# Fused cosine attention and feed-forward on one core: a ramp by quads of heads transposed on TensorE, dense chunks of 384 and 512 tokens, and each pair weighed one visit earlier

## The chip, the cores and the metric

The kernel runs on one core of a Trainium2 chip. Times are device microseconds (us) of that core. A profile's span is about 2 us shorter than the time of the run, because it counts from the first to the last instruction. Ratios are the mean time of one kernel's fast runs over that of the other's fast runs of the same rounds, so they are not quite the ratio of the medians quoted beside them.

## The reference, cut to what matters

```python
# q, k, v: (8, 12, 448, 64): batches, heads, tokens, head size; tau = 0.1
q_n = q / (norm(q) + 1e-6);  k_n = k / (norm(k) + 1e-6)
attn = softmax(q_n @ k_n.T / tau)
x = (attn @ v), heads joined              # (3584, 768)
h = x @ w_in                              # w_in (768, 2048)
out = maximum(0.01 * h, h) @ w_out        # w_out (2048, 768)
```

## The kernel before

For each batch the kernel loads q, k and v as bf16, sums squares on VectorE, takes the root on ScalarE as a logarithm and an exponential, inverts on VectorE, scales on GpSimd, and transposes q and k by DMA. Attention goes by six pairs of heads. A *visit* computes half the scores of a pair and their exponentials. *Weighing* a pair multiplies the exponentials by ones (the sums) and by v; VectorE takes the reciprocal and multiplies into x. The *dense* work is layer 1 (16 groups of matmuls for each batch) and layer 2 (56 groups in all). It is meant to fill TensorE while the next batch's attention waits for ScalarE and VectorE.

The order of all this is static. A scheduler with a clock of its own deals dense groups into the visits, and each engine then works its own list in that order:

```python
    def fill(us):
        end = clock[0] + us
        while at[0] < len(dense) and clock[0] < end:
            work, took, b = dense[at[0]]
            if done.get(b, 1e9) + 6.0 > clock[0]:   # b's attention must be over for 6 us
                break
            work(); clock[0] += took; at[0] += 1

    def prepare(b, step):            # the next batch
        if step == 0:   norm_sums(b, "q")                     # VectorE
        elif step == 1: norm_root(b, "q"); norm_sums(b, "k")  # ScalarE, VectorE
        elif step == 2: norm_inverse(b, "q"); norm_root(b, "k")
        elif step == 3: norm_inverse(b, "k"); ...scale q on GpSimd
        elif step == 4: turn(b, "q"); ...scale k on GpSimd
        elif step == 5: turn(b, "k")
        elif step == 6 and b + 1 < B: load(b + 1, "q"); load(b + 1, "k")
        elif step == 11 and b + 1 < B: load(b + 1, "v")

    last = None
    for b in range(B):
        for p in range(HP):
            for half in range(2):
                scores(b, p, half)                   # visit n = 2 * p + half
                clock[0] += 0.5
                if half == 1:
                    if last is not None:
                        weigh(*last)                 # the pair before, two visits late
                        ...
                    last = (b, p)
                prepare(b + 1, 2 * p + half)
                fill(3.0)
    # ... (functions that build the pieces, the ramp and the end are cut)
```

The last pair of batch b-1 is weighed at visit 1 of batch b, and the sums of q of batch b+1 are listed at visit 0. In VectorE's list these sums come ahead of the reciprocal of that last pair, so VectorE can do them early, while TensorE still has dense work.

## Time and profile before

| | before |
|---|---|
| time, median of 3 | 557.13 us (555.75 to 560.46) |
| span of the profile | 553.5 us |
| TensorE busy | 446.2 us (81%) |
| first score matmul | 62.7 us |
| first layer-1 matmul | 119.0 us |

These are lines of the page of the kernel before: busy time, and the span in 40 slices of 13.8 us, in tenths.

```profile
PE 446.2 (81%) x2816; PEld 216.5 (39%) x2816; DVE 265.8 (48%) x163; ACT 260.0 (47%) x409; POOL 118.3 (21%) x131
...
PE   0000285589999999499999996799999997999996
...
DVE  3600769963862536825834356836742338350000
...
PEclk9999999789999999679999999799999999999999
```

TensorE (PE) does nothing for four slices, works partly until slice 10, and is then full, except for holes about 120 us apart. In the first two of these holes the granted clock falls too. Next, what TensorE waited for, by the table of waits (us in total, times, longest):

```profile
PE sc L131 <- DMA kT<-k_n: 64.6, 2, 62.7
PE sc L131 <- ACT pe L135: 37.7, 46, 5.4
PE sm L146 <- DVE rs L153: 0.2, 1, 0.2
```

The first wait is the ramp: scores need the transposed k. No dense matmul ever waits for an eviction. The timeline of one hole (start, duration, engine, what; in brackets the idle time before it and what ended it):

```profile
217.07 0.34 ACT L93 ACTIVATE q_ni<-q_ni,tiny 112x48 f32<-112x48 f32 x1
...
221.84 3.35 DVE L87 TENSOR_REDUCE k_ni<-k_n 112x48 f32<-112x3072 bf16 x1
...
225.29 0.33 ACT L93 ACTIVATE k_ni<-k_ni,tiny 112x48 f32<-112x48 f32 x1 [5.99 <-DVE q_ni L98]
...
226.75 0.56 PE L131 MATMUL sc<-qT,kT 64*128 64x448 bf16 x2 [5.41 <-ACT pe L135]
...
238.84 4.76 PE L164 MATMUL mm<-xT,w_in_sb 128*128 128x448 bf16 x18
```

The root of k (the logarithm at L93) sat 6 us at the head of ScalarE's list, until the sum of k was done on VectorE (L87, over at 225.2; the bracket names L98, a short operation that VectorE ended at the same moment). The exponentials behind it could not start, and TensorE's scores waited 5.4 us for them. The sum of q had been done beforehand: its root ran without a wait. Dense work came back at 238.84.

### The profile page before, as it was taken

The page shows a single profiled execution, that of the slowest core. Times are in us where ns is not written, and L with a number is a line of the kernel's source. Part 1 is how long each engine was busy: PE and PEld are TensorE (multiplying, and loading weights), DVE is VectorE, ACT ScalarE, POOL GpSimd, SP SyncE. Part 2 cuts the span into 40 slices and gives each one's busy share as a digit, 9 for nine tenths or more (in the row PEclk, how much of TensorE's full clock was granted, in tenths as well). Part 3 has the DMA queues.
Part 4 walks back from the last instruction along what each step waited for, and adds up shares of the span by engine and source line. Part 5 has one row for each costly group of instructions (what it writes and reads, how often), then busy time and mean ns, then how long its engine had stood idle before and what let it go on. Part 6 is the DMA issues. An engine that isn't in the chain of part 4 may idle for free.

```text
span 553.5 us, 6672 instructions
## 1 busy us (share of the span) xinstructions
PE 446.2 (81%) x2816; PEld 216.5 (39%) x2816; DVE 265.8 (48%) x163; ACT 260.0 (47%) x409; POOL 118.3 (21%) x131
## 2 busy tenths in 40 slices
PE   0000285589999999499999996799999997999996
PEld 0000032234554454144544453244544553455553
DVE  3600769963862536825834356836742338350000
ACT  0000466467447534555546543666457437632421
POOL 3430090280055000630072000900440000000000
PEclk9999999789999999679999999799999999999999
DMA  9999829448149423392449025290560110002013
GB/s 139 216 201 188 109 54 146 50 89 114 15 103 152 67 58 76 62 138 32 73 83 167 14 66 99 51 150 1 108 128 1 40 51 25 2 1 71 16 28 86
DMA packets 83518, 45.26 MB, mean 82 GB/s; under 512 B 44832, under 2 KB 79136, under 8 KB 83488
## 3 DMA queue, kind: packets, MB, share of 16 engines
q0 software_dynamic: 35488, 22.81, 29.1%
q1 hardware_dynamic: 48000, 22.03, 19.7%
q8 instruction: 22, 0.36, 0.3%
q14 instruction: 8, 0.07, 0.0%
HBM read 45.61 MB, written 11.01 MB: 102 GB/s over the span
## 4 chain that ended last, share of the span: by engine, by line
PE 73%; DVE 9%; DMA 8%; ACT 5%; SPq 2%; POOL 1%; issue 1%; ACTq 0%; DVEq 0%; POOLq 0%
PE mm L164 27%; PE mm L180 27%; PE sm L146 7%; DMA kT<-k_n 7%; PE sc L131 6%; PE po L146 6%; ACT pe L135 5%; DVE k_ni L87 2%; DVE rs L153 2%; SPq L114 2%; DMA q_bf<-in_q_dram 1%; DVE k_n L86 1%; DVE q_ni L87 1%; POOL k_n L103 1%; DVE q_n L86 1%
## 5 line engine op out<-in xcount | busy, mean ns | idle before, releaser
L153 DVE RECIPROCAL rs<-sm 128x448 f32<-128x448 f32 x48 | 141.8, 2953 | 180.9 <-PE sm L146 180.9
L135 ACT ACTIVATE pe<-sc 112x896 bf16<-112x896 f32 x192 | 163.2, 918 | 60.9 <-PE sc L131 60.9
L164 PE MATMUL mm<-xT,w_in_sb 128*128 128x448 bf16 x768 | 153.9, 355 | 0.0
L180 PE MATMUL mm<-w_out_sb,hT 128*128 128x384 bf16 x896 | 150.1, 326 | 0.0
L131 PE MATMUL sc<-qT,kT 64*128 64x448 bf16 x384 | 62.7, 383 | 102.4 <-DMA kT<-k_n 64.6
L180 PEld LDWEIGHTS <-hT 128*128 128x128 bf16 x896 | 85.9, 98 | 63.2 <-issue 7.6
L168 ACT ACTIVATE hT<-mm 128x448 bf16<-128x448 f32 x128 | 69.8, 545 | 76.4 <-PE mm L164 76.4
L164 PEld LDWEIGHTS <-w_in_sb 128*128 128x128 bf16 x768 | 72.3, 98 | 78.2 <-issue 15.9
L185 ACT COPY osb<-mm 128x384 f32<-128x384 f32 x56 | 26.7, 477 | 110.2 <-PE mm L180 98.6
L131 PEld LDWEIGHTS <-kT 64*128 64x128 bf16 x384 | 15.0, 96 | 147.3 <-issue 81.2
L103 POOL TENSOR_TENSOR q_n<-q_bf,q_ni 112x512 bf16<-112x512 bf16 x42 | 42.3, 1038 | 80.9 <-DVE q_ni L99 80.9
L103 POOL TENSOR_TENSOR k_n<-k_bf,k_ni 112x512 bf16<-112x512 bf16 (+1 forms) x43 | 50.6, 1209 | 22.8 <-DVE k_ni L99 22.8
L146 PE MATMUL sm<-pe,ones 112*64 112x448 bf16 x384 | 51.5, 395 | 0.2 <-DVE rs L153 0.2
L146 PE MATMUL po<-pe,v_bf 112*64 112x448 bf16 x384 | 50.0, 387 | 0.0
L76 POOL DMA_DIRECT2D v_bf<-in_v_dram x8 | 7.5, 935 | 187.4 <-PE sc L131 104.0
L156 DVE TENSOR_TENSOR xT<-po,rs 128x448 bf16<-128x448 f32 x48 | 30.0, 625 | 5.4 <-PE mm L180 0.5
L86 DVE TENSOR_TENSOR q_n<-q_bf 112x3072 bf16<-112x3072 bf16 x8 | 14.0, 1751 | 37.5 <-DMA q_bf<-in_q_dram 37.5
L146 PEld LDWEIGHTS <-v_bf 112*64 112x64 bf16 x384 | 24.1, 121 | 18.1 <-issue 5.3
L146 PEld LDWEIGHTS <-ones 112*64 112x64 bf16 x384 | 19.3, 117 | 25.2 <-issue 18.9
L87 DVE TENSOR_REDUCE k_ni<-k_n 112x48 f32<-112x3072 bf16 x8 | 26.8, 3353 | 0.3
L87 DVE TENSOR_REDUCE q_ni<-q_n 112x48 f32<-112x3072 bf16 x8 | 26.8, 3353 | 0.3
L86 DVE TENSOR_TENSOR k_n<-k_bf 112x3072 bf16<-112x3072 bf16 x8 | 13.9, 1743 | 3.1 <-DMA kT<-k_n 3.1
(22 smaller groups left out, 45.4 us busy)
## 6 DMA issues: line engine op xcount, KB each, us to landing
q_bf<-in_q_dram POOLq DMA_DIRECT2D x8, 672.0 KB, 11.0
k_bf<-in_k_dram POOLq DMA_DIRECT2D x8, 672.0 KB, 13.4
v_bf<-in_v_dram POOLq DMA_DIRECT2D x8, 672.0 KB, 7.4
w_in_sb<-in_moe_w_in_dram POOLq DMA_DIRECT2D x1, 3072.0 KB, 26.3
w_out_sb<-in_moe_w_out_dram POOLq DMA_DIRECT2D x1, 3072.0 KB, 43.7
out_dram<-osb SPq DMA_DIRECT2D x8, 336.0 KB, 3.8
out_dram<-osb SPq DMA_DIRECT2D x8, 288.0 KB, 2.6
out_dram<-osb SPq DMA_DIRECT2D x8, 240.0 KB, 2.8
```

What stands on the lines that cost most here:

```text
L86: nc.vector.tensor_mul(sq, x, x)
L87: nc.vector.tensor_reduce(ni, sq, axis=AX.X, op=ALU.add)
L103: eng.tensor_tensor(out=xn[:, :, h0:h1, :].rearrange("p t h d -> p h t d"), in0=x[:, h0:h1], in1=ni[:, h0:h1].unsqueeze(3).to_broadcast([P ...
L131: nc.tensor.matmul(out=sc[:, a, :S], lhsT=kT[r, o : o + 128], rhs=q4[r, :, p, :], start=True, stop=True,)
L135: nc.scalar.activation(out=pe[:, ki], in_=sc[:PK, :, :S], func=ACTF.Exp, scale=inv_tau)
L146: nc.tensor.matmul(out=dst[64 * a : 64 * a + 64, :], lhsT=ones[:PK, :] if ones_ else vb[:, 2 * p + a, ki, :], rhs=pe[:, ki, a, :], start=( ...
L153: nc.vector.reciprocal(rs, sm)
L156: nc.vector.tensor_mul(st["x", b][:, p, :], po, rs)
L164: nc.tensor.matmul(out=pm[:, :S], lhsT=w_in_sb[:, kt, m * 128 : (m + 1) * 128], rhs=xT[:, kt, :], start=(kt == 0), stop=(kt == KT - 1),)
L168: nc.scalar.activation(out=hT[:, m, (b % 2) * S : (b % 2 + 1) * S], in_=pm[:, :S], func=ACTF.Prelu, alpha=0.01,)
L180: nc.tensor.matmul(out=po[:, :NH], lhsT=hT[:, m, i * 128 : (i + 1) * 128], rhs=w_out_sb[:, m, n * NH : (n + 1) * NH], start=(m == 0), stop ...
L185: nc.scalar.copy(out=osb[:, n * NH : (n + 1) * NH], in_=po[:, :NH])
```

## The change

There are three parts. **Ramp**: batch 0 is loaded by quads of heads, and batches 0 and 1 are normalised by quads and transposed pair by pair on TensorE, with an identity matrix; weights come in pieces; q and k loads have three shared buffers. **Chunks**: layer 1 takes 384 tokens of an even batch and 512 with the odd one, so that layer 2's tiles of 128 tokens fit whole chunks. **Order**: a pair is weighed one visit earlier, and a chunk may start 2 us, not 6, after its attention on the scheduler's clock.

```diff
 # ramp (cut)
+    make_identity(nc, ident)
+    for g in range(G):
+        for what in "qk":
+            load(0, what, 4 * g, 4 * g + 4)
+    load(0, "v")
+    prepare_quad(0, 0, nc.vector, nc.vector)     # norms of one quad
+    load(1, "q")
+    turn_pair(0, 0)                              # 8 TensorE transposes, 2 VectorE copies
+    turn_pair(0, 1)
+    visit(0, 0, 0)
+    ...
 # chunks
+    first = [7 * (c // 2) + 3 * (c % 2) for c in range(B + 1)]
+    def layer1(c, m):
+        n = 128 * (first[c + 1] - first[c])      # 384 or 512 tokens
 # order
-            if done.get(b, 1e9) + 6.0 > clock[0]:
+            if done.get(b, 1e9) + 2.0 > clock[0]:
 ...
-                if half == 1:
-                    if last is not None:
-                        weigh(*last)
-                    last = (b, p)
-                prepare(b + 1, 2 * p + half)
+                if owed:
+                    weigh(*owed.pop(0))
+                if half == 1:
+                    owed.append((b, p))
+                prepare(b + 1, n)                # b == 1 has its own list, n - 4
                 fill(3.0)
 # steps of prepare: the same up to 5, but scaling on GpSimd is listed one step earlier
 # (q at 2, k at 3); loads of q, k, v now at 6, 7 and 8
```

More of the change, by code (lines that the diff above doesn't have):

```diff
@@ L6 @@
 from concourse._compat import with_exitstack
+from concourse.masks import make_identity
 F32 = mybir.dt.float32
@@ L38 @@
     HP = H // 2
+    G = H // 4
     KT = DM // 128
@@ L46 @@
     inp = ctx.enter_context(tc.tile_pool(name="inp", bufs=1))
+    bfpool = ctx.enter_context(tc.tile_pool(name="bfpool", bufs=3))
     vpool = ctx.enter_context(tc.tile_pool(name="vpool", bufs=2))
@@ L50 @@
     wk = ctx.enter_context(tc.tile_pool(name="wk", bufs=2))
+    epool = ctx.enter_context(tc.tile_pool(name="epool", bufs=4))
+    opool = ctx.enter_context(tc.tile_pool(name="opool", bufs=4))
     xpool = ctx.enter_context(tc.tile_pool(name="xpool", bufs=2))
@@ L53 @@
     psc = ctx.enter_context(tc.tile_pool(name="psc", bufs=2, space=bass.MemoryType.PSUM))
-    ppv = ctx.enter_context(tc.tile_pool(name="ppv", bufs=1, space=bass.MemoryType.PSUM))
+    ppv = ctx.enter_context(tc.tile_pool(name="ppv", bufs=2, space=bass.MemoryType.PSUM))
     pmm = ctx.enter_context(tc.tile_pool(name="pmm", bufs=2, space=bass.MemoryType.PSUM))
@@ L62 @@
     nc.vector.memset(tiny, 1e-19)
+    ident = cpool.tile([PK, PK], BF16, name="ident")
     w_in_sb = cpool.tile([128, KT, FF], BF16, name="w_in_sb")
@@ L68, with load @@
     out_r = out.rearrange("(b p t) n -> b t p n", p=PK, t=NT)
+    w_in_r = moe_w_in.rearrange("(ko ki) n -> ki ko n", ki=128)
+    w_out_r = moe_w_out.rearrange("(mo mi) n -> mi mo n", mi=128)
     st = {}
-    def load(b, what):
+    def load(b, what, h0=0, h1=H):
         src = {"q": q_r, "k": k_r, "v": v_r}[what]
-        pool = vpool if what == "v" else inp
-        x = pool.tile([PK, H, NT, D], BF16, name=f"{what}_bf")
-        nc.gpsimd.dma_start(out=x, in_=src[b])
-        st[what, b] = x
@@ L79, in norm_sums @@
-    def norm_sums(b, what):
-        x = st[what, b]
-        xn = inp.tile([PK, NT, H, D], BF16, name=f"{what}_n")
-        ni = small.tile([PK, H, NT], F32, name=f"{what}_ni")
-        sq = xn.rearrange("p t h d -> p (t h d)").rearrange(
-            "p (h t d) -> p h t d", h=H, t=NT
-        )
-        nc.vector.tensor_mul(sq, x, x)
-        nc.vector.tensor_reduce(ni, sq, axis=AX.X, op=ALU.add)
-        st[what + "n", b] = xn
-        st[what + "i", b] = ni
-    def norm_root(b, what):
-        ni = st[what + "i", b]
+        if (what, b) not in st:
+            if what == "v":
+                st[what, b] = vpool.tile([PK, H, NT, D], BF16, name="v_bf")
+            else:
+                st[what, b] = bfpool.tile([PK, H, NT, D], BF16, name="qk_bf")
@@ new lines, in load, with load_w_in, load_w_out, norm_sums @@
+        nc.gpsimd.dma_start(out=st[what, b][:, h0:h1], in_=src[b][:, h0:h1])
+    def load_w_in(i):
+        n = slice(i * FF // 4, (i + 1) * FF // 4)
+        nc.gpsimd.dma_start(out=w_in_sb[:, :, n], in_=w_in_r[:, :, n])
+    def load_w_out(n):
+        nc.gpsimd.dma_start(
+            out=w_out_sb[:, :, n * NH : (n + 1) * NH], in_=w_out_r[:, :, n * NH : (n + 1) * NH]
+        )
+    def norm_sums(b, what, g0=0, g1=G):
+        if (what + "n", b) not in st:
+            st[what + "n", b] = inp.tile([PK, G, NT, 4, D], BF16, name=f"{what}_n")
+            st[what + "i", b] = small.tile([PK, H, NT], F32, name=f"{what}_ni")
+        x, xn, ni = st[what, b], st[what + "n", b], st[what + "i", b]
+        h0, h1 = 4 * g0, 4 * g1
+        sq = xn[:, g0:g1].rearrange("p g t h d -> p (g t h d)").rearrange(
+            "p (h t d) -> p h t d", h=h1 - h0, t=NT
+        )
+        nc.vector.tensor_mul(sq, x[:, h0:h1], x[:, h0:h1])
+        nc.vector.tensor_reduce(ni[:, h0:h1], sq, axis=AX.X, op=ALU.add)
@@ L93, in norm_root, with norm_inverse, norm_apply @@
+    def norm_root(b, what, g0=0, g1=G):
+        ni = st[what + "i", b][:, 4 * g0 : 4 * g1]
         nc.scalar.activation(ni, ni, func=ACTF.Ln, bias=tiny[:PK])
         nc.scalar.activation(ni, ni, func=ACTF.Exp, scale=0.5)
-    def norm_inverse(b, what):
-        ni = st[what + "i", b]
+    def norm_inverse(b, what, g0=0, g1=G):
+        ni = st[what + "i", b][:, 4 * g0 : 4 * g1]
         nc.vector.tensor_scalar_add(ni, ni, 1e-6)
         nc.vector.reciprocal(ni, ni)
-    def norm_apply(b, what, h0, h1, eng):
+    def norm_apply(b, what, eng, g0=0, g1=G, step=2):
@@ L102, in norm_apply @@
         x, xn, ni = st[what, b], st[what + "n", b], st[what + "i", b]
-        eng.tensor_tensor(
-            out=xn[:, :, h0:h1, :].rearrange("p t h d -> p h t d"),
-            in0=x[:, h0:h1],
-            in1=ni[:, h0:h1].unsqueeze(3).to_broadcast([PK, h1 - h0, NT, D]),
-            op=ALU.mult,
-        )
+        for h in range(4 * g0, 4 * g1, step):
+            g, a = divmod(h, 4)
+            eng.tensor_tensor(
+                out=xn[:, g, :, a : a + step, :].rearrange("p t h d -> p h t d"),
+                in0=x[:, h : h + step],
+                in1=ni[:, h : h + step].unsqueeze(3).to_broadcast([PK, step, NT, D]),
+                op=ALU.mult,
+            )
@@ L110, in turn, with turned @@
+    def turned(b, what):
+        if (what + "T", b) not in st:
+            xt = tpool.tile([128, NT * HP * PK + 16], BF16, name=f"{what}T")
+            nc.gpsimd.memset(xt[:, NT * HP * PK :], 0.0)
+            st[what + "T", b] = xt
+        return st[what + "T", b]
     def turn(b, what):
-        xn = st[what + "n", b]
-        xt = tpool.tile([128, NT * HP * PK + 16], BF16, name=f"{what}T")
-        nc.gpsimd.memset(xt[:, NT * HP * PK :], 0.0)
+        xn, xt = st[what + "n", b], turned(b, what)
@@ L114, in turn, with turn_pair @@
         nc.sync.dma_start_transpose(
             out=xt[:, : NT * HP * PK].rearrange("p (c n) -> p c n", n=PK),
-            in_=xn.rearrange("p t h d -> p (t h d)"),
+            in_=xn.rearrange("p g t h d -> p (g t h d)"),
         )
-        st[what + "T", b] = xt
+    def turn_pair(b, p):
+        g, j = divmod(p, 2)
+        tp = pmm.tile([128, 2, NT, PK], BF16, name="mm")
+        for i, what in enumerate("qk"):
+            xn = st[what + "n", b]
+            for t in range(NT):
+                nc.tensor.matmul(
+                    out=tp[:, i, t, :],
+                    lhsT=xn[:, g, t, 2 * j : 2 * j + 2, :].rearrange("p h d -> p (h d)"),
+                    rhs=ident, is_transpose=True,
+                    start=(i == 0 and t == 0), stop=(i == 1 and t == NT - 1),
+                )
+        for i, what in enumerate("qk"):
+            xt = turned(b, what)[:, : NT * HP * PK].rearrange(
+                "d (g t j n) -> d g t j n", g=G, t=NT, j=2
+            )
+            nc.vector.tensor_copy(out=xt[:, g, :, j, :], in_=tp[:, i])
@@ L120, in scores @@
     def scores(b, p, half):
         qT, kT = st["qT", b], st["kT", b]
-        q4 = qT[:, : NT * HP * PK].rearrange("d (t c n) -> d t c n", t=NT, c=HP)
+        g, j = divmod(p, 2)
+        q5 = qT[:, : NT * HP * PK].rearrange("d (g t j n) -> d g t j n", g=G, t=NT, j=2)
         if half == 0:
-            st["pe", b, p] = wk.tile([PK, NT, 2, S], BF16, name="pe")
+            st["pe", b, p] = epool.tile([PK, NT, 2, S], BF16, name="pe")
         pe = st["pe", b, p]
+        wide = 128 if b > 1 else PK
@@ L126, in scores @@
         for ki in (2 * half, 2 * half + 1):
             sc = psc.tile([128, 2, 512], F32, name="sc")
-            o = (ki * HP + p) * PK
+            o = ((g * NT + ki) * 2 + j) * PK
             for a in range(2):
@@ L131, in scores @@
                 nc.tensor.matmul(
-                    out=sc[:, a, :S], lhsT=kT[r, o : o + 128], rhs=q4[r, :, p, :],
+                    out=sc[:wide, a, :S], lhsT=kT[r, o : o + wide], rhs=q5[r, g, :, j, :],
                     start=True, stop=True,
@@ L137, in scores, with columns, x_place @@
             )
-    def weigh(b, p):
-        pe, vb = st["pe", b, p], st["v", b]
-        po = ppv.tile([128, S], F32, name="po")
-        sm = ppv.tile([128, S], F32, name="sm")
-        for dst, ones_ in ((sm, True), (po, False)):
-            for ki in range(NT):
-                for a in range(2):
-                    nc.tensor.matmul(
-                        out=dst[64 * a : 64 * a + 64, :],
-                        lhsT=ones[:PK, :] if ones_ else vb[:, 2 * p + a, ki, :],
-                        rhs=pe[:, ki, a, :],
-                        start=(ki == 0), stop=(ki == NT - 1),
-                    )
+    def columns(dst, b, p, weights):
+        for ki in range(NT):
+            for a in range(2):
+                nc.tensor.matmul(
+                    out=dst[64 * a : 64 * a + 64, :], lhsT=weights(a, ki),
+                    rhs=st["pe", b, p][:, ki, a, :],
+                    start=(ki == 0), stop=(ki == NT - 1),
+                )
+    def x_place(b):
+        if b % 2 == 0:
+            st["x", b] = xpool.tile([128, KT, 512], BF16, name="xT")
+            st["x64", b] = cpool.tile([128, KT, 64], BF16, name="x64")
+        else:
+            st["x", b] = xpool.tile([128, KT, 512], BF16, name="xT")
+            nc.gpsimd.tensor_copy(out=st["x", b][:, :, 0:64], in_=st["x64", b - 1])
+    def weigh(b, p):
+        vb = st["v", b]
+        sm = ppv.tile([128, S], F32, name="pv")
+        columns(sm, b, p, lambda a, ki: ones[:PK, :])
         rs = wk.tile([128, S], F32, name="rs")
@@ L154, in weigh @@
         if p == 0:
-            st["x", b] = xpool.tile([128, KT, S], BF16, name="xT")
-        nc.vector.tensor_mul(st["x", b][:, p, :], po, rs)
-    def layer1(b, m):
-        if b % 2 == 0 and m == 0:
-            st["h", b // 2] = hpool.tile([128, MT, 2 * S], BF16, name="hT")
-        hT, xT = st["h", b // 2], st["x", b]
+            x_place(b)
+        po = ppv.tile([128, S], F32, name="pv")
+        columns(po, b, p, lambda a, ki: vb[:, 2 * p + a, ki, :])
+        x = st["x", b]
+        if b % 2 == 0:
+            nc.vector.tensor_mul(x[:, p, 0:384], po[:, 0:384], rs[:, 0:384])
+            nc.vector.tensor_mul(st["x64", b][:, p, :], po[:, 384:S], rs[:, 384:S])
+        else:
+            nc.vector.tensor_mul(x[:, p, 64:512], po, rs)
+    first = [7 * (c // 2) + 3 * (c % 2) for c in range(B + 1)]
+    def layer1(c, m):
+        n = 128 * (first[c + 1] - first[c])
+        if m == 0:
+            st["h", c] = hpool.tile([128, MT, 512], BF16, name="hT")
         pm = pmm.tile([128, 512], F32, name="mm")
@@ L164, in layer1, with layer2 @@
             nc.tensor.matmul(
-                out=pm[:, :S], lhsT=w_in_sb[:, kt, m * 128 : (m + 1) * 128],
-                rhs=xT[:, kt, :], start=(kt == 0), stop=(kt == KT - 1),
+                out=pm[:, :n], lhsT=w_in_sb[:, kt, m * 128 : (m + 1) * 128],
+                rhs=st["x", c][:, kt, :n], start=(kt == 0), stop=(kt == KT - 1),
             )
         nc.scalar.activation(
-            out=hT[:, m, (b % 2) * S : (b % 2 + 1) * S], in_=pm[:, :S],
-            func=ACTF.Prelu, alpha=0.01,
-        )
-    def layer2(b2, i, n):
-        hT = st["h", b2]
-        if n == 0:
-            st["o", b2, i] = wk.tile([128, DM], F32, name="osb")
-        osb = st["o", b2, i]
+            out=st["h", c][:, m, :n], in_=pm[:, :n], func=ACTF.Prelu, alpha=0.01
+        )
+    def layer2(c, i, n):
+        j0 = (i - first[c]) * 128
         po = pmm.tile([128, 512], F32, name="mm")
@@ L180, in layer2 @@
             nc.tensor.matmul(
-                out=po[:, :NH], lhsT=hT[:, m, i * 128 : (i + 1) * 128],
+                out=po[:, :NH], lhsT=st["h", c][:, m, j0 : j0 + 128],
                 rhs=w_out_sb[:, m, n * NH : (n + 1) * NH],
@@ L184, in layer2 @@
             )
-        nc.scalar.copy(out=osb[:, n * NH : (n + 1) * NH], in_=po[:, :NH])
-        if n == 1:
-            j, end = i * 128, (i + 1) * 128
-            while j < end:
-                bb, c = divmod(j, S)
-                t, p0 = divmod(c, PK)
-                n_ = min(end - j, PK - p0)
-                nc.sync.dma_start(
-                    out=out_r[2 * b2 + bb, t, p0 : p0 + n_, :],
-                    in_=osb[j - i * 128 : j - i * 128 + n_, :],
-                )
-                j += n_
+        osb = opool.tile([128, NH], F32, name="osb")
+        nc.scalar.copy(out=osb, in_=po[:, :NH])
+        j, end = i * 128, (i + 1) * 128
+        while j < end:
+            b, col = divmod(j, S)
+            t, p0 = divmod(col, PK)
+            w = min(end - j, PK - p0)
+            nc.sync.dma_start(
+                out=out_r[b, t, p0 : p0 + w, n * NH : (n + 1) * NH],
+                in_=osb[j - i * 128 : j - i * 128 + w, :],
+            )
+            j += w
     dense = []
-    for b in range(B):
+    for c in range(B):
         for m in range(MT):
-            dense.append((lambda b=b, m=m: layer1(b, m), 1.13, b))
-        tiles = range(0, 3) if b % 2 == 0 else range(3, 7)
-        for i in tiles:
-            for n in range(2):
-                dense.append((lambda b=b, i=i, n=n: layer2(b // 2, i, n), 2.6, b))
+            t1 = 6 * (128 * (first[c + 1] - first[c]) / 2400 + 0.005)
+            dense.append((lambda c=c, m=m: layer1(c, m), t1, c))
+        tiles = [(i, n) for i in range(first[c], first[c + 1]) for n in range(2)]
+        if c == 0:
+            tiles.sort(key=lambda x: x[1])
+        for i, n in tiles:
+            dense.append((lambda c=c, i=i, n=n: layer2(c, i, n), 2.65, c))
     done = {}
@@ L220, in fill @@
             at[0] += 1
-    for what in "qkv":
-        load(0, what)
-    nc.gpsimd.dma_start(out=w_in_sb, in_=moe_w_in.rearrange("(ko ki) n -> ki ko n", ki=128))
-    nc.gpsimd.dma_start(out=w_out_sb, in_=moe_w_out.rearrange("(mo mi) n -> mi mo n", mi=128))
-    for what, eng in (("q", nc.vector), ("k", nc.gpsimd)):
-        norm_sums(0, what)
-        norm_root(0, what)
-        norm_inverse(0, what)
-    for what, eng in (("k", nc.gpsimd), ("q", nc.vector)):
-        norm_apply(0, what, 0, H, eng)
@@ L234 @@
-    for what in "qk":
-        turn(0, what)
-    for what in "qkv":
-        load(1, what)
-    def prepare(b, step):
-        if b >= B:
-            return
-        if step == 0:
-            norm_sums(b, "q")
-        elif step == 1:
-            norm_root(b, "q")
-            norm_sums(b, "k")
-        elif step == 2:
-            norm_inverse(b, "q")
-            norm_root(b, "k")
-        elif step == 3:
-            norm_inverse(b, "k")
-            for h in range(0, H, 2):
-                norm_apply(b, "q", h, h + 2, nc.gpsimd)
-        elif step == 4:
-            turn(b, "q")
-            for h in range(0, H, 2):
-                norm_apply(b, "k", h, h + 2, nc.gpsimd)
-        elif step == 5:
-            turn(b, "k")
-        elif step == 6 and b + 1 < B:
-            load(b + 1, "q")
-            load(b + 1, "k")
-        elif step == 11 and b + 1 < B:
-            load(b + 1, "v")
@@ L268, with prepare_quad @@
-    last = None
-    for b in range(B):
+    make_identity(nc, ident)
[3 more added lines that the diff above has]
+    load(0, "v")
+    def prepare_quad(b, g, eq, ek):
+        for what in "qk":
+            norm_sums(b, what, g, g + 1)
+            norm_root(b, what, g, g + 1)
+        for what, eng in (("q", eq), ("k", ek)):
+            norm_inverse(b, what, g, g + 1)
+            norm_apply(b, what, eng, g, g + 1, 4 if eng is nc.vector else 2)
@@ new lines, in visit @@
+    def visit(b, p, half):
+        scores(b, p, half)
+        clock[0] += 0.5
+    prepare_quad(0, 0, nc.vector, nc.vector)
[3 more added lines that the diff above has]
+    visit(0, 0, 0)
+    prepare_quad(0, 1, nc.gpsimd, nc.vector)
+    load_w_in(0)
+    load_w_in(1)
+    visit(0, 0, 1)
+    turn_pair(0, 2)
+    visit(0, 1, 0)
+    turn_pair(0, 3)
+    visit(0, 1, 1)
+    prepare_quad(0, 2, nc.gpsimd, nc.gpsimd)
+    load(1, "k")
+    load_w_in(2)
+    load_w_in(3)
+    visit(0, 2, 0)
@@ new lines @@
+    weigh(0, 0)
+    visit(0, 2, 1)
+    turn_pair(0, 4)
+    weigh(0, 1)
+    visit(0, 3, 0)
+    turn_pair(0, 5)
+    visit(0, 3, 1)
+    load_w_out(0)
+    load(1, "v")
+    load_w_out(1)
+    visit(0, 4, 0)
+    weigh(0, 2)
+    visit(0, 4, 1)
+    weigh(0, 3)
+    visit(0, 5, 0)
+    prepare_quad(1, 0, nc.gpsimd, nc.gpsimd)
+    visit(0, 5, 1)
+    weigh(0, 4)
+    weigh(0, 5)
+    done[0] = clock[0]
+    clock[0] += 2.0
+    load(2, "q")
+    turn_pair(1, 0)
+    turn_pair(1, 1)
+    fill(4.0)
@@ new lines, in prepare @@
+    def prepare(b, step):
+        if b < B:
+            if step == 0:
+                norm_sums(b, "q")
+            elif step == 1:
+                norm_root(b, "q")
+                norm_sums(b, "k")
+            elif step == 2:
+                norm_inverse(b, "q")
+                norm_root(b, "k")
+                norm_apply(b, "q", nc.gpsimd)
+            elif step == 3:
+                norm_inverse(b, "k")
+                norm_apply(b, "k", nc.gpsimd)
+            elif step == 4:
+                turn(b, "q")
+            elif step == 5:
+                turn(b, "k")
+            if step == (7 if b == 2 else 8):
+                load(b, "v")
+        if b + 1 < B:
+            if step == 6:
+                load(b + 1, "q")
+            elif step == 7:
+                load(b + 1, "k")
@@ L270 @@
+    owed = []
+    for b in range(1, B):
         for p in range(HP):
@@ L273 @@
                 clock[0] += 0.5
-                if half == 1:
-                    if last is not None:
-                        weigh(*last)
-                        clock[0] += 1.6
-                        if last[1] == HP - 1:
-                            done[last[0]] = clock[0]
-                    last = (b, p)
-                prepare(b + 1, 2 * p + half)
+                if owed:
+                    w = owed.pop(0)
+                    weigh(*w)
+                    clock[0] += 1.6
+                    if w[1] == HP - 1:
+                        done[w[0]] = clock[0]
+                if half == 1:
+                    owed.append((b, p))
+                n = 2 * p + half
+                if b == 1:
+                    if n == 0:
+                        prepare_quad(1, 1, nc.gpsimd, nc.gpsimd)
+                    elif n == 1:
+                        turn_pair(1, 2)
+                        prepare_quad(1, 2, nc.gpsimd, nc.gpsimd)
+                        load(2, "k")
+                    elif n <= 4:
+                        turn_pair(1, n + 1)
+                    prepare(b + 1, n - 4)
+                else:
+                    prepare(b + 1, n)
                 fill(3.0)
-    weigh(*last)
+    for w in owed:
+        weigh(*w)
     done[B - 1] = clock[0]
-    fill(6.0)
-    clock[0] += 6.0
+    clock[0] += 3.0
     fill(1e9)
```

## The prediction

> **What bounds the kernel now.** The page gives PE 446 us busy of 553.5. From the timeline, warm steady costs are: a visit (scores of half a pair) 0.48 us, a weighing 1.63, a layer-1 group of 448 tokens 1.17, a layer-2 group 2.65. Times 96, 48, 128 and 56 that is about 422 us of TensorE work. The other 131 us are: first score matmul at 62.7 us (chain of waits: transposes by DMA landing beside weight loads, the longest wait on PE); then no dense work until 119 us; then holes at 217 to 239, 337 to 359 and 456 to 469 us (table of windows), where the static order has run out of dense work: about 15, 14 and 5 us lost; and a 4.7 us tail. In the first two holes VectorE is full (three reciprocals of 2.95 us plus sums of squares, 5.1 us per tensor), and ScalarE stands behind a logarithm waiting for those sums, so exponentials stop (waits of 5.4 us).
>
> **Removed.** Four DMA transposes in the ramp, and the wait for whole batches. **Added.** 96 TensorE transposes. The Trainium skill ("TensorE: Matmul & The Clock Gate", PE-mode transpose) gives 275 to 390 ns for one alone; no trace here shows it, and pipelined I estimate 0.1 us, 10 us in all. Each pair adds two VectorE copies from PSUM, 0.4 to 0.6 us each, an estimate from the 0.62 us multiply of the same size. Layer 1 saves about 2 us; extra output DMAs cost nothing.
>
> **Ramp.** VectorE works through it alone: scaling the 1.75 and 3.35 us durations to a quad gives 1.9 us per tensor; six reciprocals and multiplies take 22 us; copies, norms and the first quad of batch 1 fill the rest. First scores at about 17 us, attention of batch 0 over and dense work starting at about 60 us (before: 119).
>
> **Given back.** Chunk 0 alone is available then. Counting the static order, dense work ends after visit 5 of batch 1; visits 6 to 11 have none, and batch 2 waits for its norms (GpSimd 6 us per tensor) and DMA transposes. Dense work resumes for good at about 150 us, at a point that before reached at 165: some 15 us gained, not 60.
>
> Later the order leaves visits 9 to 11 of odd batches and 0 and 1 of every batch without dense work. Weighing of the last pair now precedes the next sums on VectorE, so both sums, and the roots that block ScalarE's evictions, fall in the hole: about 9 us lost at the start of odd batches, 13 at odd to even, 22 per two batches where before lost 15. With the end, about 50 us against 32. The walk ends at 550 to 565 us. Intent and tuned constants argue for somewhat less than the walk.
>
> **Prediction.** 555 us (before 557), 8 in 10 between 536 and 573. Faster by over 2%: 0.29; within 2%: 0.54; slower: 0.17. On the critical path: the ramp's VectorE queue, then TensorE's floor plus the holes.
>
> **What would show each step.** Right: first score matmul at 14 to 20 us; first layer-1 matmul at 55 to 65 us with VectorE over 85% busy before it; a TensorE hole of over 20 us around 110 to 150 us; thereafter two holes per two batches, each ending with ScalarE's logarithm released by VectorE's sum; TensorE busy time within 15 us of before's. Wrong: dense work continuous after 60 us; layer 1 waiting for weights; transposes over 0.2 us apiece; no stall at visits 0 to 2.
>
> **What would make it wrong.** If sums overtake the reciprocals in practice, holes shrink and 535 is possible. If the norms of batch 2 on GpSimd slip, or weight loads (issued behind waiting GpSimd work) arrive after 60 us, the ramp gain vanishes and it is slower.

## The result, and the profile after

The changed kernel took 585.27 us (median of 4, 582.51 to 587.37), against 557.67 for the kernel before. The ratio is 1.049, with a 95% interval from 1.042 to 1.055. It is slower. All outputs are right.

| | before | after |
|---|---|---|
| span | 553.5 us | 583.2 us |
| TensorE busy | 446.2 us | 471.2 us |
| mean granted clock | 0.965 | 0.918 |
| first score matmul | 62.7 us | 14.0 us |
| first layer-1 matmul | 119.0 us | 66.0 us |
| layer 1 of batch 2 under way | 165.3 us | 162.0 us |
| from there to the end | 388.2 us | 421.2 us |

The fourth and fifth rows are what the change was for, and they came out. The sixth compares nearly like points: the attention of batch 2 at its first visits (four done before, three after), chunk 0 of the dense work complete, chunk 1 just begun (one group done before, two after). A lead of 53 us at the first dense matmul had shrunk to 3 us there, and then 33 us were lost. Even some of the 3 us is how the points differ: the new chunk 0 is 64 tokens shorter, about 2.7 us of layer 1 (an estimate from the 1.17 us of a group of 448 tokens). Lines of the page of the changed kernel (slices of 14.6 us):

```profile
PE 471.2 (81%) x2912; PEld 229.8 (39%) x2912; DVE 280.5 (48%) x245; ACT 265.5 (46%) x425; POOL 127.4 (22%) x150
...
PE   1686769960589994998589993999579999996996
...
DVE  5878743880952249324953239422954224434000
...
PEclk9985889965879998999979998899969999999999
```

There are now two holes where before had one in the same stretch, and a bottomless one (0) in slice 10. TensorE's waits in the changed kernel:

```profile
PE mm L233 <- ACT hT L237: 42.5, 8, 8.1
PE sc L180 <- ACT pe L184: 22.0, 36, 2.9
PE sc L180 <- DMA kT<-k_n: 13.5, 1, 13.5
PE mm L154 <- DVE q_n L126: 11.1, 1, 11.1
```

The first line is new: layer 1 stops because ScalarE has not emptied PSUM. The timeline at the start of batch 3 shows why:

```profile
219.50 0.95 PE L191 MATMUL pv<-pe,ones 112*64 112x448 bf16 x8
...
220.04 1.75 DVE L109 TENSOR_TENSOR q_n<-qk_bf 112x3072 bf16<-112x3072 bf16 x1
...
221.13 2.12 PE L233 MATMUL mm<-xT,w_in_sb 128*128 128x384 bf16 x12
221.83 3.35 DVE L110 TENSOR_REDUCE q_ni<-q_n 112x48 f32<-112x3072 bf16 x1
225.10 1.75 DVE L109 TENSOR_TENSOR k_n<-qk_bf 112x3072 bf16<-112x3072 bf16 x1
225.27 0.33 ACT L114 ACTIVATE q_ni<-q_ni,tiny 112x48 f32<-112x48 f32 x1 [6.12 <-DVE q_ni L110]
...
226.88 3.35 DVE L110 TENSOR_REDUCE k_ni<-k_n 112x48 f32<-112x3072 bf16 x1
...
230.33 0.33 ACT L114 ACTIVATE k_ni<-k_ni,tiny 112x48 f32<-112x48 f32 x1 [2.83 <-DVE k_ni L110]
...
230.84 0.85 ACT L237 ACTIVATE hT<-mm 128x384 bf16<-128x384 f32 x2
231.37 3.69 PE L233 MATMUL mm<-xT,w_in_sb 128*128 128x384 bf16 x12 [8.11 <-ACT hT L237]
```

VectorE finishes the last pair of batch 2 (at about 220) and only then starts both sums, from 220.04 to 230.2. ScalarE stands at the root of q (6.1 us), then at the root of k (2.8 us). Layer 1 has two PSUM buffers, so TensorE does two groups (12 matmuls) and stops for 8.1 us, until the first evictions at 230.84. The Trainium skill ("TensorE: Matmul & The Clock Gate", the table at its head) calls ScalarE's queue a strict FIFO; these lines agree: an eviction ready since about 222 us waited behind a logarithm. After the stall 12 such matmuls took 3.69 us in place of 2.12: the same page (Part 1) says that an idle window of about 3.4 us brings the half clock back, and the trace agrees (the mean granted clock was 1.00 up to 226.7 us, and 0.56 from 231.4 to 235.0).

The other loss is in the ramp. Of the timeline of the changed kernel, GpSimd's and SyncE's queue and the first scores of batch 2:

```profile
128.66 6.04 POOL L126 TENSOR_TENSOR k_n<-qk_bf,k_ni 112x512 bf16<-112x512 bf16 x6
...
134.73 3.41 SPq L143 DMA_TRANSPOSE kT<-k_n  x1
134.74 0.98 POOL L88 DMA_DIRECT2D qk_bf<-in_q_dram  x1
...
144.36 0.93 PE L180 MATMUL sc<-qT,kT 64*128 64x448 bf16 x4 [13.52 <-DMA kT<-k_n]
```

TensorE waits 13.5 us for kT of batch 2. The transpose was issued at 134.7 and landed 9.6 us later; three loads were issued in the 2 us after it.

### The profile page after: what moved, and what is told of

Same layout as the page of the kernel before. It is cut to its first block, busy times and chain, and to the rows that moved or that the text cites. A ratio compares the mean times of both kernels' runs of the same rounds, so it can differ in the third digit from the quotient of the medians.

```text
span 583.2 us, 7085 instructions
## 1 busy us (share of the span) xinstructions
PE 471.2 (81%) x2912; PEld 229.8 (39%) x2912; DVE 280.5 (48%) x245; ACT 265.5 (46%) x425; POOL 127.4 (22%) x150
## 4 chain that ended last, share of the span: by engine, by line
PE 58%; DVE 10%; issue 3%; ACT 3%; DMA 2%; ACTq 0%; DVEq 0%; POOL 0%
PE mm L245 23%; PE mm L233 23%; PE pv L191 8%; PE sc L180 5%; DVE rs L212 4%; DVE k_ni L110 3%; ACT pe L184 2%; DMA kT<-k_n 2%; DVE k_n L109 2%; DVE q_n L109 1%; ACT hT L237 0%; ACT osb L251 0%; ACT k_ni L114 0%; ACT k_ni L115 0%; DVE xT L222 0%
## 5 line engine op out<-in xcount | busy, mean ns | idle before, releaser
L212 DVE RECIPROCAL rs<-pv 128x448 f32<-128x448 f32 x48 | 141.7, 2952 | 230.0 <-PE pv L191 229.9
L233 PE MATMUL mm<-xT,w_in_sb 128*128 128x384 bf16 (+1 forms) x768 | 164.4, 369 | 46.7 <-ACT hT L237 42.5
L237 ACT ACTIVATE hT<-mm 128x384 bf16<-128x384 f32 (+1 forms) x128 | 68.9, 544 | 93.3 <-PE mm L233 93.0
L126 POOL TENSOR_TENSOR q_n<-qk_bf,q_ni 112x512 bf16<-112x512 bf16 x46 | 46.5, 1041 | 234.0 <-DVE k_ni L119 147.5
L180 PE MATMUL sc<-qT,kT 64*128 64x448 bf16 (+1 forms) x384 | 65.3, 400 | 35.6 <-ACT pe L184 22.0
L191 PE MATMUL pv<-pe,ones 112*64 112x448 bf16 x384 | 52.2, 399 | 7.8 <-DVE rs L212 7.8
L191 PE MATMUL pv<-pe,v_bf 112*64 112x448 bf16 x384 | 51.6, 395 | 0.0
L126 POOL TENSOR_TENSOR k_n<-qk_bf,k_ni 112x512 bf16<-112x512 bf16 x44 | 44.4, 1042 | 0.0
L110 DVE TENSOR_REDUCE k_ni<-k_n 112x16 f32<-112x1024 bf16 (+1 forms) x12 | 27.4, 2286 | 0.4
L110 DVE TENSOR_REDUCE q_ni<-q_n 112x16 f32<-112x1024 bf16 (+1 forms) x12 | 27.4, 2286 | 0.4
L109 DVE TENSOR_TENSOR q_n<-qk_bf 112x1024 bf16<-112x1024 bf16 (+1 forms) x12 | 14.6, 1216 | 4.2 <-DMA qk_bf<-in_q_dram 4.2
## 6 DMA issues: line engine op xcount, KB each, us to landing
qk_bf<-in_k_dram POOLq DMA_DIRECT2D x7, 672.0 KB, 12.3
```

The costliest lines, as they stand in the source:

```text
L109: nc.vector.tensor_mul(sq, x[:, h0:h1], x[:, h0:h1])
L110: nc.vector.tensor_reduce(ni[:, h0:h1], sq, axis=AX.X, op=ALU.add)
L126: eng.tensor_tensor(out=xn[:, g, :, a : a + step, :].rearrange("p t h d -> p h t d"), in0=x[:, h : h + step], in1=ni[:, h : h + step].unsq ...
L180: nc.tensor.matmul(out=sc[:wide, a, :S], lhsT=kT[r, o : o + wide], rhs=q5[r, g, :, j, :], start=True, stop=True,)
L191: nc.tensor.matmul(out=dst[64 * a : 64 * a + 64, :], lhsT=weights(a, ki), rhs=st["pe", b, p][:, ki, a, :], start=(ki == 0), stop=(ki == NT ...
L212: nc.vector.reciprocal(rs, sm)
```

## The experiments

One theory stood at the start, with three rivals. **H**: the order is the loss. It puts the sums of the next batch into a hole without dense work, where ScalarE's roots wait for them and hold up evictions. Rivals: **C**, the unequal chunks make the holes; **V**, VectorE's time itself, not the roots, stops TensorE; **R**, the ramp with its transposes and copies is the loss. **D** is an addition: loads beside the transpose of k delay batch 2.

### One part alone, and parts undone

**e8_order_alone**: the kernel before, with the order part alone.

```diff
-            if done.get(b, 1e9) + 6.0 > clock[0]:
+            if done.get(b, 1e9) + 2.0 > clock[0]:
...
-                if half == 1:                       # weigh the pair before, two visits late
-                    if last is not None: weigh(*last) ...
+                if owed: weigh(*owed.pop(0)) ...    # one visit late
+                if half == 1: owed.append((b, p))
...                                                  # and at the end of the last batch:
-    fill(6.0)
-    clock[0] += 6.0
+    clock[0] += 3.0
```

> The kernel before with one part of the change alone: each pair is weighed one visit earlier and the dense chunk of a batch may start 2 us (not 6) of the scheduler's count after its last weighing. Ramp, chunks of 448 and everything else are those of before. H' (the order is the loss: it puts the last weighing ahead of the next batch's first sums and leaves visits 0 and 1 of every batch without dense work, so both sums fall into a hole in every batch): 572 to 590 us, with TensorE stalls of 6 to 8 us before layer 1, released by an eviction, in each of batches 1 to 6. If the order is harmless and the loss needs the ramp or the chunks: 550 to 562 us.

Measured: 591.96 us, ratio 1.067 (1.061 to 1.074), just above the range expected. Its waits of TensorE now have the line that before lacked (the first wait, of 71 us, is for the old ramp's transposes and, once, for those of batch 1):

```profile
PE sc L131 <- DMA kT<-k_n: 71.2, 2, 62.7
PE mm L164 <- ACT hT L168: 44.4, 6, 7.8
```

The order alone costs 36 us, more than the whole change does. H holds, and ramp and chunks are not needed for the loss.

**e12_lag_alone**: the kernel before with only the first line of that diff (6.0 to 2.0).

> The kernel before with the shorter lag alone (a chunk may start 2 us of the scheduler's count after its last weighing, not 6); weighing stays where it was. By the static order this alone turns the one long hole in every second batch into a shorter one at the start of every batch, but the last weighing stays behind the next batch's first sums, which VectorE can then do early. If the lag is the loss and the earlier weighing adds little: 580 to 592 us. If the loss needs the earlier weighing, which puts both sums inside the hole: 552 to 565. If both share: 566 to 579.

Measured: 570.92 us, ratio 1.032 (1.022 to 1.043). The same stalls are there, shorter:

```profile
PE mm L164 <- ACT hT L168: 18.5, 6, 4.3
```

Both halves of the order share the loss. The shorter lag gives every batch a hole at its start (18 us lost). Weighing a visit earlier puts the sums of q, too, behind the last pair in VectorE's list, and the stalls grow from at most 4.3 to 7.8 us (about 20 us more).

**e3_equal_chunks**: the changed kernel with 448 tokens a chunk, as before.

```diff
-        n = 128 * (first[c + 1] - first[c])
+        n = S
 ... (x of one batch, hidden tile of two batches, as before)
-    epool bufs=4, opool bufs=4
+    epool bufs=3, opool bufs=2        # to fit
```

> The changed kernel with layer 1 in chunks of 448 tokens, one per batch, as before (x of one batch, hidden tile of two batches; to fit, three buffers of exponentials and two of outputs in place of four). Rival C (unequal chunks leave five visits without dense work at odd to even): most of the loss goes, 560 us or less. H: the hole lies at visits 0 and 1 of every batch whatever the chunks are, with the sums in it; the stall before even batches gets shorter by two or three visits' latency, layer 1 costs 2 us more: 575 to 588 us, stalls of 6 to 8 us in every batch.

Measured: 568.93 us, ratio 1.023 (1.020 to 1.026), below the range expected by H, with 42.5 us of stalls before layer 1 as in the changed kernel:

```profile
PE mm L224 <- ACT hT L228: 42.5, 8, 7.8
```

So the chunks cost about 15 us on top, more than I had allowed, and a rival that blamed them alone falls: the stalls stay. The 15 us hold behind the new ramp; behind the old one, e4 (below, 1.075) and e8 (1.067), which differ in buffers and in the place of the loads too, are only some 4 us apart, and no run says why. By the static order the 384-token chunk runs out after visit 8 of odd batches, so five visits in a row have no dense work; with equal chunks there are three.

**e4_old_ramp**: the changed kernel with batch 0 loaded, normalised and DMA-transposed whole, and batch 1 prepared like the others.

```diff
-    (ramp by quads)
+    for what in "qkv": load(0, what)
+    ... weights; norms of whole q and k; turn(0, "q"); turn(0, "k"); loads of batch 1
-    for b in range(1, B):
+    for b in range(B):
```

> The changed kernel with the ramp of before: batch 0 loaded whole, normalised whole, transposed by DMA; batch 1 prepared as the others; the steady order and the chunks stay changed. My reading of the traces: the new ramp brings dense work to 66 us but runs out of it, and its resumption after batch 1 at 162 us compares with about 172 here: 590 to 602 us, that is, the new ramp is worth 7 to 17 us. Rival R1 (the ramp is worth what its first dense matmul suggests, 40 us or more): 620 us or more. Rival R2 (the ramp is itself the loss: transposes, copies, quads): 575 us or less.

Measured: 597.87 us, ratio 1.075 (1.072 to 1.078), inside the expectation. The new ramp is a gain, but of 13 us (14 by the ratios), not of the 53 us by which dense work starts sooner. R falls.

### Inside the hole

**e1_roots_later**: the changed kernel; for batches 3 to 7 the sums stay at visits 0 and 1, and roots, scaling and transposes come about three visits later.

```diff
-            elif step == 1: norm_root(b, "q"); norm_sums(b, "k")
-            elif step == 2: norm_inverse(b, "q"); norm_root(b, "k"); ...
+            elif step == 1: norm_sums(b, "k")
+            elif step == 4: norm_root(b, "q"); norm_root(b, "k")
+            elif step == 5: (inverses and scaling)    # transposes at 7 and 8
```

> For batches 3 to 7 the sums of squares stay where they are (visits 0 and 1), but ScalarE's roots, and all that follows from them, move three visits later. Theory H (the roots in ScalarE's queue wait for the sums and hold up the evictions of layer 1, so TensorE stops): the five TensorE stalls of 6.6 to 8.1 us before layer 1, released by an eviction, disappear, 37 us, and with them some 8 us of matmuls at the low clock after each stall: 538 to 550 us, TensorE busy time down by about 8 us. Rival V (VectorE itself is short in the hole: the reciprocals stand behind the sums and that is what stops TensorE): 573 us or more, the stalls turn into waits for reciprocals. Rival C (the unequal chunks make the hole): no change, 580 to 588 us.

Measured: 565.1 us, ratio 1.015 (1.012 to 1.019). Its waits of TensorE:

```profile
PE pv L191 <- DVE rs L212: 23.8, 9, 7.3
...
PE sc L180 <- DMA kT<-k_n: 17.5, 2, 13.3
...
PE mm L233 <- ACT hT L237: 5.0, 3, 3.5
```

The stalls on evictions went from 42.5 to 5.0 us, so the roots were what stopped layer 1. But only 20 of some 45 us came back, and the 538 to 550 us expected were missed. Waits for reciprocals rose from 7.8 to 23.8 us: with the roots gone the sums still stand ahead of the reciprocals. V is the next limit, not a false theory.

**e2_sums_later**: the whole preparation three visits later.

```diff
-                    prepare(b + 1, n)
+                    prepare(b + 1, n - 3)
```

> From batch 2 on, all steps of preparing the next batch (sums, roots, scaling, transposes, loads) come three visits later, so the sums fall among dense work and not in the hole. H and V both: the same five stalls disappear, and reciprocals in the hole are not delayed either: 530 to 545 us, a little below the run with only the roots moved if VectorE matters too, equal within 5 us if it doesn't. Rival C: 578 us or more. If the later transposes arrive too late for the next batch, TensorE waits for kT at visit 0 of each batch and the gain is smaller.

Measured: median 571.63 us, from 564.5 to 578.4; by its fast runs 1.017 (1.012 to 1.022), which is about 566 us, and not the 530 to 545 expected. The holes at odd batches closed, but TensorE waited for kT 28.3 us in three places in place of 13.5 in one: the expectation's last sentence came true. The transpose of k of batch 4 stood behind output DMAs in SyncE's list until 248.8 us, so that the three loads left just before it (245.7 to 247.6 us), and it landed after 18.5 us.

### Loads beside a transpose

**e6_loads_first** and **e11_loads_apart**: the changed kernel with loads moved, nothing else.

```diff
             elif step == 1:
+                load(b, "v")
+                load(b + 1, "q")      # e11; in e6 this one is at step 0
...
-            if step == 6: load(b + 1, "q")   (k at 7, v at 8)
             elif step == 2:
                 norm_inverse(b, "q"); norm_root(b, "k"); norm_apply(b, "q", nc.gpsimd)
+                load(b + 1, "k")
```

> The changed kernel; only the place of the loads changes: v of the next batch and q of the one after are issued with the sums, k of the one after between the scaling of q and that of k, so no load is issued together with the transpose of k. Theory D (q, k and v loads share the DMA engines with the transpose, which makes kT land after 9.5 us in place of about 4, and the 13.5 us wait at the start of batch 2 is partly that): kT lands in 3.5 to 6 us, the wait at batch 2 is 7 to 9 us, the total 575 to 581. If the transpose itself takes that long: landing and total unchanged.

> The changed kernel with loads moved only, and better than in e6_loads_first, where the q load of the following batch still went out half a microsecond after the transpose of k: here v and that q load are issued behind a wait that keeps them clear of it. Theory D: kT of batch 2 lands in about 5.3 us (9.6 in the changed kernel), TensorE's wait for it falls from 13.5 to about 10 us, the total to 579 to 583 us. If landing time doesn't follow the loads: 9 us and 13.5 us as before.

In e6 the q load of the batch after still left GpSimd 0.5 us after the transpose, so it was no test. In e11 no load left in the 7 us before it, or after it until it had landed. The issues of DMA between 100 and 150 us (the last figure is us from issue to landing) of the changed kernel, e6 and e11 in turn:

```profile
kT<-k_n SPq DMA_TRANSPOSE x1, 9.6
```

```profile
kT<-k_n SPq DMA_TRANSPOSE x1, 9.3
```

```profile
kT<-k_n SPq DMA_TRANSPOSE x1, 4.5
```

D holds for the landing: one load issued beside it is enough to bring it to 9.3 us (in e5, below, where only this load is away, it is 5.3), and three make it 9.6. The Trainium skill ("DMA: Bandwidth & Descriptors", Queues, rings and completion order) says that each DMA engine goes round its queues packet by packet; that fits, and the page gives no figure for it. For the total D is small: e6 took 587.07 us (1.057, 1.049 to 1.065), e11 582.27 us (1.050, 1.044 to 1.057), neither different from the changed kernel. In e11 the wait fell from 13.5 to 9.5 us, but its transpose was issued 4 us later (139.1 in place of 134.7), so scores of batch 2 began at 143.6 in place of 144.4.

**e5_sums_late_loads**: e2 and the moved loads together.

> The run with all preparation three visits later, and the loads ahead of the scaling of k as in the run beside it. There kT landed after 18 us and TensorE waited for it 28 us in three places. D: kT lands in 3.5 to 6 us, those waits shrink to one of 7 to 9 us in the ramp, the total is 538 to 548 us: below before. If the wait comes from the later scaling and not from the loads: kT waits stay above 15 us in all, total above 555.

Measured: 547.8 us, ratio 0.986 (0.977 to 0.994). The waits for kT fell from 28.3 to 10.3 us, in one place. In that position the loads mattered; in the changed kernel, where kT has time to spare from batch 3 on, they didn't. This is the first version whose interval lies below 1, though by less than 2%.

### Mending the order

**e7_even_dense**: e5, and dense groups dealt by a running account.

```diff
-        end = clock[0] + us
-        while at[0] < len(dense) and clock[0] < end:
+        credit[0] += us
+        while at[0] < len(dense) and credit[0] > 0:
             ...                                   # each group is taken from the credit
-                fill(3.0)
+                fill(3.3)
```

> The same, and the dense groups handed out by a running account of 3.3 us a visit in place of at least 3.0 at every visit, so that a chunk lasts until about the next one may start. If holes are what is left to lose: 522 to 536 us, TensorE busy above 88% of the span, and no hole of over 5 us after 160 us. If the holes left cost nothing, or the order now delays something else: within 5 us of the run beside it.

Measured: 545.33 us, ratio 0.983 (0.976 to 0.989): no different from e5. The second reading was right: evening out uncovered eviction stalls (24.0 us against 16.7), and the next run tests whether roots listed too close behind their sums are the cause.

**e9_best**: e7, with each root one visit later than there, which is two visits behind its sum, and k of batch 2 scaled on VectorE.

```diff
             elif step == 1:
-                norm_root(b, "q")
                 norm_sums(b, "k")
             elif step == 2:
+                norm_root(b, "q")
                 norm_inverse(b, "q")
-                norm_root(b, "k")
 ...
             elif step == 3:
+                norm_root(b, "k")
                 norm_inverse(b, "k")
-                norm_apply(b, "k", nc.gpsimd)
+                norm_apply(b, "k", nc.vector if b == 2 else nc.gpsimd)    # in steps of 4 or 2 heads
```

> e7_even_dense with ScalarE's two roots put one visit behind their sums, and k of batch 2 scaled on VectorE beside q on GpSimd. Theory H: the stalls of 3.5 to 4.4 us before layer 1, released by an eviction, in each batch disappear (about 20 us), the wait for kT at batch 2 falls from 12.3 to about 5 us: 515 to 530 us, against 545. If these stalls only uncover the next wait (reciprocals, exponentials): 535 to 545.

Measured: 519.98 us, ratio 0.938 (0.932 to 0.944). TensorE's row of its page (slices of 13 us):

```profile
PE   0587386995399999999999999999999999998996
```

There is no hole after the ramp. Its stalls on evictions are 6.0 us in all:

```profile
PE mm L233 <- ACT hT L237: 6.0, 5, 3.5
```

The wait for kT at batch 2 fell only to 8.7 us, not to 5: landing took 9.5 us here again (the k load of the next batch had left 3.0 us before the transpose and was still in flight). That part of the expectation missed.

**e10_best_old_ramp**: the order of e9 behind the old ramp (diff as in e4, with e9's steps and dealing).

> The order of e9_best behind the ramp of before (batch 0 whole, DMA transposes). The ramp was worth 13 us with the order of the changed kernel. If it is worth about the same in a good order: 10 to 22 us slower than e9_best, 530 to 550. If a bad order had hidden its worth: 35 us or more slower than e9_best.

Measured: 526.26 us, ratio 0.949 (0.944 to 0.955), 6 us slower than e9 in the same rounds. The expectation of 10 to 22 us was too high: in a good order the new ramp gives 6 us. The good order with the new chunks, but the old ramp, is 28 us faster than the kernel before.

| kernel | ramp | chunks | order | median, us | ratio |
|---|---|---|---|---|---|
| before | old | 448 | old | 557.1 | 1 |
| e12_lag_alone | old | 448 | lag only | 570.9 | 1.032 |
| e8_order_alone | old | 448 | new | 592.0 | 1.067 |
| e4_old_ramp | old | 384/512 | new | 597.9 | 1.075 |
| e3_equal_chunks | new | 448 | new | 568.9 | 1.023 |
| the change | new | 384/512 | new | 585.3 | 1.049 |
| e10_best_old_ramp | old | 384/512 | mended | 526.3 | 0.949 |
| e9_best | new | 384/512 | mended | 520.0 | 0.938 |

## Why the prediction was wrong

The mechanisms were named and came true, and the time still fell outside the range (536 to 573): the walk left out one stall, at batch 2, and set unlike losses side by side in the batches after it.

- *What bounds the kernel*: right. TensorE's holes, VectorE's sums and the waiting logarithm are what the runs showed too.
- *Ramp*: near. First scores at 14.0 us (17 predicted), first dense matmul at 66.0 us (about 60; the range given, 55 to 65, was just missed), VectorE 83% busy between 6 and 66 us (over 85%). Copies took 0.38 us (0.4 to 0.6). Eight transposes took 0.45 us at full clock, 0.06 each.
- *"Dense work resumes for good at about 150 us, at a point that before reached at 165: some 15 us gained"*: this step failed. Layer 1 of batch 2 did start at 152.66, but not for good: after two groups it stood for 6.6 us behind an eviction, by the same roots, and was under way only at 162.0, a gain of 3.3 us. The walk had such stalls at the later batches and none here. e1 shows it: there the roots of batch 3 come later, and layer 1 goes straight on, though the first scores of batch 2 are no earlier (145.25 us against 144.36). The changed kernel, then e1:

```profile
152.66 2.76 PE L233 MATMUL mm<-xT,w_in_sb 128*128 128x512 bf16 x12
161.99 2.72 PE L233 MATMUL mm<-xT,w_in_sb 128*128 128x512 bf16 x6 [6.57 <-ACT hT L237]
```

```profile
152.98 4.06 PE L233 MATMUL mm<-xT,w_in_sb 128*128 128x512 bf16 x18
```

  The rest of the 12 us missing is that batch 2 was late. Its kT took 9.6 us to land, where e6's expectation has about 4 (the prediction gives no figure); e11 shows that loads beside it make that difference, but also that mending it alone is given back by a later issue. That GpSimd ends the scaling of k only at 134.7 us is read from the trace and was not tested alone.
- *"22 per two batches where before lost 15. With the end, about 50 us against 32"*: this step failed in size. I had 18 us more loss after the resumption, and it was 33.0: TensorE idle for 52.5 us in place of 25.9, and busy for 6.4 us more. From one stall of layer 1 to the same one two batches later took 131.9 us (161.99 to 293.85), where the kernel before took 119.8 for two batches: 12 us more, not 7. The changed kernel, then the kernel before:

```profile
162.00:293.85 131.85, 111.18 (x704) 53.53 (x704) 65.34 (x47) 64.73 (x103) 31.75 (x35) 0.94 0.44 74
```

```profile
119.04:238.84 119.80, 111.36 (x706) 53.45 (x705) 66.37 (x41) 64.31 (x102) 31.73 (x37) 0.94 0.50 81
```

  The figures are the length, the busy times of PE, PEld, DVE, ACT and POOL, then the granted clock and the DMA. TensorE is busy for 111 us at a mean clock of 0.94 in both, so the 12 us are idle time: 20.7 us in place of 8.4. The stalls are its largest part (8.1 us at odd batches, 7.3 before even ones). The walk's 22 was thus near the idle time alone. Its 15 for the kernel before was near the whole loss against the warm costs, low clock included: 119.8 less 105.6 is 14.2 (an estimate from the prediction's costs for 24 visits, 12 weighings, 32 and 14 dense groups). Each kernel is busy for some 6 us more than the warm costs in two batches, and only the 15 seems to have had them in it; that is inferred from the sizes, since the record doesn't say how the 15 and the 22 were reckoned. The low clock is real (after each stall 6 to 12 matmuls took 1.3 to 1.6 us longer), but over two batches it costs the changed kernel no more than the kernel before.
- *"Intent and tuned constants argue for somewhat less than the walk"*: this step had no measurement behind it. The walk ended at 550 to 565, and I moved the estimate to 555.
- *TensorE busy time within 15 us of before's*: wrong. It rose by 25.0 us: layer 1 by 10.5, for as many columns as before (a saving of 2 was predicted), and the two groups of transposes by some 11. Of the 25.0, 18.6 came before 162 us, where the mean granted clock was 0.82 (0.96 before).
- *What would make it wrong*: for the slow side I had named weights after 60 us and late norms of batch 2. The weights were in time; batch 2 was late.

The sum: 553.5 - 3.3 + 33.0 = 583.2. Mine was 553.5 - 15 + 18 = 556.5.

Shown by runs: the order costs 36 us alone (e8), half of it by the lag (e12); the new ramp is worth 6 us in the mended order (e9 against e10), 13 to 14 in the changed order (the change against e4) and some 24 there with equal chunks (e3 against e8, by their ratios); the unequal chunks cost about 15 us in this order behind the new ramp (e3) and some 4 behind the old (e4 against e8); stalls on evictions come from the roots (e1), and with sums, roots and loads put apart and dense work dealt evenly the same parts give 520 us (e9). Left open: how the 25 us from e7 to e9 divide between its two edits (stalls on evictions fell from 24.0 to 6.0 us, the wait for kT from 12.3 to 8.7), why the chunks cost less behind the old ramp, and the share of the low clock in the ramp.

## What to carry to other kernels

A lead in the ramp is worth only what the steady state lets it keep: compare two traces at a point of equal work done, not at the first busy matmul. Where each engine works a fixed list, a short operation that waits (here a logarithm of 48 columns) stops everything behind it on its engine, so list it behind its producer by as long as the producer takes, and list what it needs ahead of work that only the hole can feed. When fill work runs out before the next may start, deal it by an account that lasts until then, and check what falls into each gap that remains.

## What the Trainium skill lacked or had wrong

- "TensorE: Matmul & The Clock Gate", Part 4, gives 390 ns for a lone 128x128 bf16 transpose and about 275 ns in a kernel. In the changed kernel one transpose of 112x128 lasted 255 to 261 ns on average by the trace, near the second figure; but eight in a row, between layer-1 matmuls, took 0.45 us (77.01 to 77.46), 56 ns each. The page has no figure for the spacing of transposes in a row.
- "DMA: Bandwidth & Descriptors" gives the rule by which queues share an engine but no figure for a transpose beside a load. Here the transpose of k of batch 2 (112x3072 bf16) landed after 4.5 to 5.3 us with no load issued in the 7 us before it or until it landed (e11, e5), and after 9.3 to 9.6 us with one or three loads of 672 KB issued in the 2 us after it (e6, the changed kernel). With three loads issued in the 3 us before it, one took 18.5 us (e2, batch 4).
- No page read for this case says what a waiting root in ScalarE's list costs TensorE. Here two PSUM buffers of layer 1 covered 2.1 us, and the stall was 8.1 us.
